# Loading u and v in DMAs of two token tiles each, in a fused attention and maxout kernel

## The chip, the cores and the metric

The kernel runs on one core of a Trainium2 chip. The metric is the device time of one execution in microseconds. A core has five engines that run side by side: TensorE (PE, the matrix unit, with its weight loads shown as PEld), VectorE (DVE), ScalarE (ACT), GpSimd (POOL) and SyncE (SP). POOL and SP also issue the DMAs, which 16 DMA engines carry out.

## The reference

Eight batches of 3072 tokens go through a gated attention without softmax and then through a two-way maxout layer:

```python
scores = (1.0 / S) * np.matmul(z, z.transpose(0, 2, 1))   # z: [8, 3072, 64]
attn = np.maximum(scores, 0.0) ** 2
x = (u * np.matmul(attn, v)).reshape(B * S, D)            # u, v: [8, 3072, 256]
h1, h2 = x @ w1, x @ w2                                   # [256, 1024] each
out = np.maximum(h1, h2) @ w_out                          # [1024, 256]
```

All inputs and the output are float32.

## The kernel before

**Tiling.** A batch is 24 token tiles of 128 tokens. Token `p * 24 + t` lies in partition `p` of tile `t` (`by_tile`, line 68), so neighbouring tiles are neighbours in one partition's row in memory. Four tiles make a group (`G`), two groups a couple: six groups and three couples to a batch. Everything that PE reads is bfloat16. Loads of u, v and z convert on the way in, and POOL issues them.

**u** comes by group: `load_u` (line 181) fills a tile `un` of 128 x 4 x 256 from two buffers in turn, with one DMA. `turn_u` (line 185) then has SP transpose it by DMA into `uT`, which `gate` (line 420) multiplies with the attention's result.

**v** comes in pieces of eight tiles, three pieces a batch, in five buffers: `load_v` (line 151) fills tiles `lo` to `lo + n` of a piece with one DMA. By default that is the whole piece; at the start the first batch's pieces are loaded in parts of 2, 2 and 4 tiles and then of 4. PE reads v as the weights of the attention's product (lines 279 and 892), and DVE's `combine_v` (line 164) forms the differences that the Strassen form needs.

**z** is loaded by `load_z`, except for the first batch, whose z comes in through SP as float32 and is cast by ACT, DVE and, for tiles 12 to 23, POOL (`double_first`, line 118; six casts). PE then transposes it (`zT_pe`, line 122).

**Scores** are made in pairs of token tiles: two matmuls (line 211), a relu on ACT or DVE (lines 222 and 224), a square on DVE (lines 230 and 232). The score matrix is symmetric, so blocks of 512 x 512 above the diagonal are computed and SP mirrors them by DMA transposes (`mirror`, line 261; line 235 inside a diagonal block).

**Stages.** Groups 0 to 3 of the first batch are done plainly, one at a time (loop at line 605). The couple of groups 4 and 5, `i == 2` in the loop at line 740, is the plain couple: four accumulators, two of them on each half of PE's rows at a time, in 96 steps. The 21 couples of the other batches use a Strassen-Winograd form of seven products on 2 x 2 blocks, in 84 steps. After each couple `second` (line 686) runs the maxout layer of the couple before (`ff`, line 435), and its hooks place DVE's work for the next couple.

**Order.** The order of instructions on each engine is written out by hand; semaphores are added from the data that instructions share. In the couples a list `plan` places loads and transposes at step numbers (lines 824 to 866), for example

```python
if i == 2:
    plan = [
        (1, turn_u, 0, 4),
        (4, turn_u, 0, 5),
        (12, load_v, 1, 0),
        (16, load_v, 1, 1),
        (36, load_v, 1, 2),
    ]
```

An accumulator is first added to on one half of PE's rows and later on the other. Between the two, a relay, an instruction that does nothing but wait for the first half's last matmul, has to run on another engine: on POOL in the plain couple, on ACT in all others (line 873). The matmul of the second half waits for the relay (line 904). At a step the relays that are due come before the loads placed there.

POOL's queue therefore holds, in this order of issue: at the start, seven loads of v, the identity matrix, two loads of u, the six casts of z; later the weights, z, u and v, the relays of the plain couple, and all output DMAs (line 476) but the last ten, which SP issues.

Of the kernel before, what the change touches and what calls it, by code (L numbers as in the profile page):

```python
# [11 lines left out]
def kernel(  # L12
# [10 lines left out]
    nc = tc.nc  # L23
# [12 lines left out]
    G = 4  # L36
# [31 lines left out]
    def by_tile(x):  # L68
        return x.rearrange("(p t) d -> p t d", t=NT)
# [81 lines left out]
    def load_v(b, piece, lo=0, n=2 * G, held=False):  # L151
        if (b, piece) not in vp:
            vp[b, piece] = vpool.tile([P, 2 * G, D], bf16, name="v_sb")
        t = vp[b, piece]
        if held:
            nc.vector.memset(t[:, lo, 0:1], 0.0)
        nc.gpsimd.dma_start(
            out=t[:, ds(lo, n), :], in_=by_tile(v[b])[:, ds(piece * 2 * G + lo, n), :]
        )

    def v_at(b, t, dc):
        return vp[b, t // (2 * G)][:, t % (2 * G), ts(dc, P)]
# [16 lines left out]
    un, uT = {}, {}  # L179

    def load_u(b, g):
        un[b, g] = unat.tile([P, G, D], bf16, name="un")
        nc.gpsimd.dma_start(out=un[b, g], in_=by_tile(u[b])[:, ds(g * G, G), :])

    def turn_u(b, g):
        t = upool.tile([P, G, KD, P], bf16, name="uT")
# [360 lines left out]
    def need(b, g, n):  # L547
        most = pair_at[b, g, 2 * g]
        for t in range(n + 1):
            if t // G >= g:  # L550
                most = max(most, pair_at[b, g, t // 2] + 1)
        return most

    with tc.manual_schedule():
# [3 lines left out]
        nc.vector.memset(warm, 0.0)  # L558
        vp[0, 2] = vpool.tile([P, 2 * G, D], bf16, name="v_sb")
        load_v(0, 0, 0, 2)  # L560
        make_identity(nc, ident)
        load_v(0, 0, 2, 2)
        load_v(0, 0, G, G)
        for piece in range(1, NC):
            for lo in (0, G):
                load_v(0, piece, lo, G)
        load_u(0, 0)
        load_u(0, 1)
        z_first += [Block(), Block()]
        w1, w2, w2T = Block(), Block(), Block()  # L570
# [34 lines left out]
        for i in range(PLAIN):  # L605
            b, g = groups[i]
# [3 lines left out]
            for slot, (n, dc) in enumerate(steps_of(i)):  # L610
                tick += 1
                k = need(b, g, n)
# [16 lines left out]
                if i in (1, 2) and n in (5, 8):  # L629
                    k = n // 8  # L630
# [8 lines left out]
                if i + 1 < PLAIN:  # L639
                    if i and n == 1:  # L640
                        load_u(*groups[i + 1])
                    if n == (13 if i == 2 else 16):
                        turn_u(*groups[i + 1])
                if (i, n) in ((0, 20), (1, 10)):
                    w_in = ((w2_sb, moe_w2), (w1_sb, moe_w1)) if i == 0 else ((w_out_sb, moe_w_out),)
                    nc.vector.memset(w_in[0][0][:, 0, 0:1], 0.0)
                    for w_sb, w in w_in:
                        nc.gpsimd.dma_start(
                            out=w_sb, in_=w.rearrange("(c p) f -> p c f", p=P)
# [79 lines left out]
        b, g = groups[PLAIN - 1]  # L729
# [10 lines left out]
        for i in range(PLAIN // 2, len(couples)):  # L740
            b, c = couples[i]
# [3 lines left out]
                b, c, forms, blocks=PLAIN_COUPLES.get(i)  # L745
# [178 lines left out]
        b, c = couples[-1]  # L924
# [31 lines left out]
```

## Time and profile before

| | |
|---|---|
| median of 6 runs | 914.4 us (910.59 to 920.24) |
| the profiled execution | 912.66 us |
| its span, first to last instruction | 910.9 us |
| granted PE clock, mean over the span | 0.998 |
| PE busy | 902.1 us, 99% |
| DVE, ACT, POOL busy | 724.0, 602.0, 105.7 us |
| packets of POOL's DMA queue | 22,592, 52.57 MB, 29.1% of 16 engines' span |
| packets of SP's DMA queue | 359,040, 91.79 MB, 59.8% |
| u loads: number, KB each, us from issue to landing | 48, 256 KB, 6.2 |
| v loads | 21 of 512 KB, 7.2; 5 of 256 KB, 7.3; 2 of 128 KB, 4.6 |

A row of the profile names the engine, the source line, the operation, the tiles (out <- in), the shapes and the count; after the bar come busy time and mean duration, then the engine's idle time before these instructions and what ended it. In the waits, `A L1 <- B L2: 5.0, 3, 2.0` reads: A, before its instruction of line 1, was idle 5.0 us in all in 3 places, 2.0 at most, until B's instruction of line 2 was done. In the stretches each engine's busy time stands with its number of instructions in brackets; then follow the granted clock of PE as a share of full speed, the mean busy share of the 16 DMA engines (packets overlap, so it can pass 1) and the rate. KB are counted as they arrive in the core's memory, so u and v, which halve on the way, take twice that from HBM.

### The profile page before, as it was taken

To read this page: it belongs to the slowest core of one execution; us is meant where nothing else is said; L and a number is where in the kernel's file an instruction comes from. 1 tells how busy PE (TensorE), PEld (TensorE's weight loads), DVE (VectorE), ACT (ScalarE), POOL (GpSimd) and SP (SyncE) were. 2 spreads that over 40 slices of the span, in tenths; PEclk is the share of its full clock that TensorE was granted. 3 is DMA by queue.
4 is the path that set the end of the run, shared out by engine and by line. 5 is a ranking of instruction groups with operands and counts; after the bars stand their busy time and mean duration, and the time that the engine had idled before them with its cause. 6 is when DMAs were issued, how large, how long until landed. Compare 5 with 4: busy or idle time off the path is not lost.

```text
span 910.9 us, 19275 instructions
## 1 busy us (share of the span) xinstructions
PE 902.1 (99%) x7526; PEld 519.8 (57%) x7526; DVE 724.0 (79%) x1093; ACT 602.0 (66%) x1191; POOL 105.7 (12%) x200
## 2 busy tenths in 40 slices
PE   8999999999999999999999999999999999999998
PEld 3456465565565655665656656566465564655655
DVE  6782689779998799887997979979799788995640
ACT  6887966667666676667666666666766567673445
POOL 3101010110110111101111012010110110100000
PEclk9999999999999999999999999999999999999999
DMA  9999989889798895998969999798988979887201
GB/s 190 153 200 205 204 162 171 153 169 191 137 190 146 177 187 112 205 158 165 166 118 204 155 168 180 148 192 148 166 177 143 193 150 181 153 163 142 74 24 71
DMA packets 381724, 145.60 MB, mean 160 GB/s; under 512 B 360256, under 2 KB 364992, under 8 KB 381632
## 3 DMA queue, kind: packets, MB, share of 16 engines
q1 hardware_dynamic: 359040, 91.79, 59.8%
q0 software_dynamic: 22592, 52.57, 29.1%
q8 instruction: 59, 0.97, 0.4%
q14 instruction: 33, 0.27, 0.1%
HBM read 59.77 MB, written 25.17 MB: 93 GB/s over the span
## 4 chain that ended last, share of the span: by engine, by line
PE 97%; DVE 2%; ACT 1%; issue 0%; ACTq 0%; DVEq 0%
PE acc L892 45%; PE d_ps L440 18%; PE o_ps L463 18%; PE s_ps L211 7%; PE o_ps L454 5%; PE acc L279 3%; DVE blk L232 1%; ACT r_sb L224 0%; PE acc L583 0%; DVE blk L230 0%; PE w2o_ps L672 0%; DVE xT L424 0%; DVE w_sb L655 0%; ACT zT L129 0%; PE tpz L125 0%
## 5 line engine op out<-in xcount | busy, mean ns | idle before, releaser
L892 PE MATMUL acc<-blk,v_sb 64*128 64x512 bf16 x2208 | 450.4, 376 | 0.0
L224 ACT ACTIVATE r_sb<-s_ps 128x512 bf16<-128x512 f32 (+3 forms) x672 | 335.9, 559 | 123.3 <-PE s_ps L211 81.9
L892 PE MATMUL acc<-blk,vt 64*128 64x512 bf16 x1512 | 364.1, 376 | 0.0
L892 PEld LDWEIGHTS <-v_sb 64*128 64x128 bf16 x2208 | 176.1, 94 | 133.9 <-issue 6.2
L232 DVE TENSOR_TENSOR blk<-r_sb 128x1024 bf16<-128x1024 bf16 x257 | 172.2, 687 | 92.0 <-ACT r_sb L224 91.0
L447 ACT ACTIVATE g_sb<-d_ps 128x512 bf16<-128x512 f32 x384 | 193.3, 630 | 28.5 <-PE d_ps L440 28.3
L463 PE MATMUL o_ps<-w_out_sb,g_sb 128*128 128x256 bf16 x1536 | 175.5, 273 | 0.0
L892 PEld LDWEIGHTS <-vt 64*128 64x128 bf16 x1512 | 139.2, 94 | 63.0
L440 PE MATMUL d_ps<-xT,w_sb 128*128 128x512 bf16 x768 | 173.9, 379 | 0.0
L463 PEld LDWEIGHTS <-g_sb 128*128 128x128 bf16 x1536 | 150.3, 98 | 17.4
L475 ACT COPY o_sb<-o_ps 128x512 f32<-128x512 f32 (+1 forms) x98 | 56.4, 577 | 132.4 <-PE o_ps L463 132.4
L767 DVE TENSOR_TENSOR h_sb<-h_sb,acc 128x512 f32<-128x512 f32 x168 | 109.3, 681 | 28.7 <-ACT h_sb L771 20.9
L211 PE MATMUL s_ps<-zT 64*128 64x512 bf16 (+3 forms) x676 | 126.4, 360 | 2.4 <-DVE zT L129 1.8
L440 PEld LDWEIGHTS <-w_sb 128*128 128x128 bf16 x768 | 73.3, 98 | 89.3 <-issue 9.7
L476 POOL DMA_DIRECT2D out_dram<-o_sb x88 | 48.1, 546 | 561.6 <-ACT o_sb L475 561.6
L335 DVE TENSOR_TENSOR blk<-blk,blk 128x2048 bf16<-128x2048 bf16 x63 | 77.2, 1225 | 2.1
L331 DVE TENSOR_TENSOR blk<-blk,blk 128x2048 bf16<-128x2048 bf16 x63 | 76.7, 1217 | 0.0
L782 DVE TENSOR_TENSOR blk<-blk,blk 128x2048 bf16<-128x2048 bf16 x63 | 76.5, 1217 | 0.0
L339 DVE TENSOR_TENSOR blk<-blk,blk 128x2048 bf16<-128x2048 bf16 x63 | 73.2, 1217 | 2.5 <-DMA blk<-blk 2.5
L424 DVE SCALAR_TENSOR_TENSOR xT<-h_sb,uT 128x512 bf16<-128x512 f32 x96 | 61.9, 683 | 4.7 <-PE o_ps L454 4.7
L230 DVE TENSOR_TENSOR blk<-r_sb 128x512 bf16<-128x512 bf16 (+3 forms) x162 | 48.3, 334 | 20.2 <-ACT r_sb L224 19.2
L211 PEld LDWEIGHTS <-zT 64*128 64x128 bf16 x676 | 36.0, 94 | 40.7 <-DVE zT L129 2.4
(48 smaller groups left out, 317.1 us busy)
## 6 DMA issues: line engine op xcount, KB each, us to landing
out_dram<-o_sb POOLq DMA_DIRECT2D x88, 256.0 KB, 3.6
un<-in_u_dram POOLq DMA_DIRECT2D x48, 256.0 KB, 6.2
v_sb<-in_v_dram POOLq DMA_DIRECT2D x21, 512.0 KB, 7.2
blk<-blk SPq DMA_TRANSPOSE x240, 4.8
zn<-in_z_dram POOLq DMA_DIRECT2D x21, 128.0 KB, 4.0
out_dram<-o_sb SPq DMA_DIRECT2D x6, 256.0 KB, 2.0
v_sb<-in_v_dram POOLq DMA_DIRECT2D x5, 256.0 KB, 7.3
blk<-in_moe_w_dram POOLq DMA_DIRECT2D x2, 512.0 KB, 6.4
```

The costliest lines, as they stand in the source:

```text
L211: nc.tensor.matmul(s_ps[h][:, lo[h] :], zT[rows, z_at(b, blk * G + tiles[h]), :], zT[rows, q + lo[h] // P : q + G, :].rearrange("p t c -> ...
L224: nc.scalar.activation(o, s, AF.Relu)
L232: nc.vector.tensor_mul(a[:, k : k + 2, :], r, r)
L331: nc.vector.tensor_add(*alike(f["S1"], f["A21"], f["A22"]))
L335: nc.vector.tensor_sub(*alike(f["S2"], f["S1"], f["A11"]))
L339: nc.vector.tensor_sub(*alike(f["S3"], f["A11"], f["A21"]))
L440: nc.tensor.matmul(d_ps, w15_sb[:, kc, ts(nb, P)], xT[:, kc, :], start=(kc == 0), stop=(kc == KD - 1),)
L447: nc.scalar.activation(g_sb[:, nb, :], d_ps, AF.Relu)
L463: nc.tensor.matmul(o_ps[t // 2][:, t % 2, :], g_sb[:, nb, ts(t, P)], w_out_sb[:, nb, :], start=False, stop=(nb == KF - 1 and t % 2 == 1),)
L767: nc.vector.tensor_add(out, a, b_)
L782: nc.vector.tensor_sub(f["A12"].ap, f["A12"].ap, f["S2"].ap)
L892: mm = nc.tensor.matmul(a.out(acc[name]), w()[rows], a.moving(rows, j), start=name not in opened, stop=left[name] == 0,)
```

## The change

Both load functions issue one DMA for every two token tiles, so that one DMA brings 1 KB (2 x 256 bfloat16 values) to each partition. A load of u is two DMAs, a load of a whole piece of v four, a load of half a piece two; the two loads of two tiles at the start stay as they are. Tiles, buffers, places in the order and the waits for a buffer to come free are the same; all DMAs of a load follow one another on POOL.

```diff
@@ -154,9 +154,10 @@
         t = vp[b, piece]
         if held:
             nc.vector.memset(t[:, lo, 0:1], 0.0)
-        nc.gpsimd.dma_start(
-            out=t[:, ds(lo, n), :], in_=by_tile(v[b])[:, ds(piece * 2 * G + lo, n), :]
-        )
+        for k in range(lo, lo + n, 2):
+            nc.gpsimd.dma_start(
+                out=t[:, ds(k, 2), :], in_=by_tile(v[b])[:, ds(piece * 2 * G + k, 2), :]
+            )
@@ -180,7 +181,10 @@
     def load_u(b, g):
         un[b, g] = unat.tile([P, G, D], bf16, name="un")
-        nc.gpsimd.dma_start(out=un[b, g], in_=by_tile(u[b])[:, ds(g * G, G), :])
+        for k in range(0, G, 2):
+            nc.gpsimd.dma_start(
+                out=un[b, g][:, ds(k, 2), :], in_=by_tile(u[b])[:, ds(g * G + k, 2), :]
+            )
```

## The prediction

> **What bounds the kernel now.** I read first the page's busy times and the shares of the chain that ended last, then the waits of TensorE (PE) alone, then GpSimd's (POOL's) groups, because every DMA of the change is issued there, then the start and the one stretch in which PE waits for POOL.
>
> Busy times and chain, from the page:
>
> ```profile
> span 910.9 us, 19275 instructions
> PE 902.1 (99%) x7526; PEld 519.8 (57%) x7526; DVE 724.0 (79%) x1093; ACT 602.0 (66%) x1191; POOL 105.7 (12%) x200
> PE 97%; DVE 2%; ACT 1%; issue 0%; ACTq 0%; DVEq 0%
> ```
>
> PE is the bound from 53 us to the end: 910.9 - 902.1 = 8.8 us are all that any change can give back without shortening matmuls, and the waits of PE alone say that 4.8 us of these lie in the first 53 us:
>
> ```profile
> PE s_ps L211 <- DVE zT L129: 1.8, 1, 1.8
> PE acc L583 <- DVE blk L558: 1.2, 1, 1.2
> PE s_ps L211 <- ACT zT L129: 0.6, 1, 0.6
> PE acc L279 <- DVE blk L232: 0.4, 1, 0.4
> ```
>
> No wait of PE names a DMA. POOL's groups show the price of issuing a load, and what POOL waits for:
>
> ```profile
> L476 POOL DMA_DIRECT2D out_dram<-o_sb x88 | 48.1, 546 | 561.6 <-ACT o_sb L475 561.6
> L183 POOL DMA_DIRECT2D un<-in_u_dram x48 | 26.1, 550 | 97.4 <-DMA uT<-un 96.8 <-issue 0.5
> L157 POOL DMA_DIRECT2D v_sb<-in_v_dram x28 | 15.5, 556 | 41.7 <-PE acc L892 33.6 <-PE s_ps L211 7.3 <-POOLq L940 0.8
> L120 POOL CAST blk<-z 128x256 bf16<-128x256 f32 x6 | 2.3, 481 | 0.0
> ```
>
> POOL is idle for 88% of the span. Two places are not idle time: the start, where six casts that PE needs stand behind nine loads, and the plain couple (84 to 107 us), whose relays (line 873) POOL runs. In time order, POOL and the Vector engine (DVE) at the start:
>
> ```profile
> 2.46 3.21 POOL L157 DMA_DIRECT2D v_sb<-in_v_dram  x6
> 5.63 1.10 POOL L183 DMA_DIRECT2D un<-in_u_dram  x2
> 6.68 2.35 POOL L120 CAST blk<-z 128x256 bf16<-128x256 f32 x6
> 5.95 2.83 DVE L230 TENSOR_TENSOR blk<-r_sb 128x512 bf16<-128x512 bf16 x2
> ```
>
> and the stretches of the granted clock there (columns: stretch, sum of busy time, then PE, PEld, DVE, ACT, POOL, the clock, the DMA share, GB/s):
>
> ```profile
> 6.76:10.17 3.41, 1.57 (x16) 0.71 (x16) 3.21 (x3) 1.40 (x3) 2.27 (x6) 1.00 1.08 189
> 10.17:13.59 3.42, 3.42 (x20) 1.22 (x18) 2.09 (x4) 2.34 (x5) 0.00 (x0) 0.50 1.11 206
> 13.59:17.00 3.41, 2.85 (x30) 1.16 (x26) 1.65 (x3) 2.39 (x4) 0.00 (x0) 1.00 1.19 210
> ```
>
> After a stretch with PE busy 1.57 of 3.41 us the clock is 0.50 for 3.41 us; after one with 2.85 it stays 1.00. Last, POOL's loads in the plain couple and the relays of all couples:
>
> ```profile
> 87.05 0.54 POOL L157 DMA_DIRECT2D v_sb<-in_v_dram  x1 [2.53 <-PE s_ps L211]
> 88.13 0.54 POOL L157 DMA_DIRECT2D v_sb<-in_v_dram  x1 [0.54 <-PE acc L892]
> 93.39 0.53 POOL L157 DMA_DIRECT2D v_sb<-in_v_dram  x1 [4.72 <-PE s_ps L211]
> ...
> L873 ACTq EVENT_SEMAPHORE  x126: 17/17/17, 128.2 to 870.5; - x126
> L873 POOLq EVENT_SEMAPHORE  x44: 17/17/17, 84.2 to 106.8; - x44
> ```
>
> **The change part by part.** *Count.* 48 loads of u become 96; of the 28 loads of v, 21 whole pieces become four each (+63), five half pieces two each (+5), two loads of two tiles stay. That is 116 more DMAs, 116 x 0.55 = 64 us of POOL. They lie in the 561.6 us that POOL waits for o_sb: each burst of loads starts right after an output DMA, and the next output comes 5 us or more later (22 to 25 us in most cases). Cost 0 there. If that cover were gone, an output would be late by at most the 3 + 1 + 1 extra issues of a burst, 2.7 us.
>
> *The relays.* In the plain couple PE repeats every 1.08 us: the last matmuls of two accumulators on one half of the array, then POOL's two relays, then the matmuls on the other half that wait for them. One by one, the trace has relays at 84.23 and 84.32 and the waiting matmuls at 84.90, so the second relay may be 0.58 us late. Loads of v stand in POOL's order after the relays of steps 12, 16 and 36. Behind the relay of 86.48 the load's record begins at 87.05, 0.57 later; loads in a row begin 0.53 apart (the start above: 3.21 us for six), and POOL's sequencer is held until the last has begun. Today that is free by 87.05, ahead of the next relays at 87.47 and 87.56. With four loads it is free at 0.57 + 3 x 0.53 = 2.16 us after the relay, the second relay comes at 2.25, and PE wants it at 1.08 + 0.58 = 1.66: PE stalls 0.6 us. The load of step 16 stands behind those late relays: its own next pair comes 2.25 after them, while PE, which resumed on them, wants it 1.08 later: 1.2 us. The load of step 36 stands alone again: 0.6. Sum 2.4 us. Bounds: 0 if queued DMAs do not hold the sequencer (the single loads here do not delay a relay); above, each POOL DMA carries one of eight semaphores in turn and waits for the eighth before it. The last DMA of the step 16 load would wait for the output issued at 83.97, which landed 6.0 us later, at 89.96; its turn is about 90.3. Were that landing 1 us later, 0.7 more. So 0 to 3.1, and I take 2.4, by the row that is nearest.
>
> *The start.* POOL now issues 9 loads by 6.15 and then the casts. It will issue 16 ahead of them, and the last waits for the landing of the eighth. Loads of 256 KB landed 1.25 us apart here (8.87 to 15.13 us), the second of the 128 KB ones at 7.36, so the eighth lands at 7.36 + 6 x 0.63 = 11.1, or 12.0 if each takes 0.78. The casts then begin at 12.2 to 13.1 and the fourth ends 1.5 later, at 13.7 to 14.6; PE's transposes that need it ran at 14.21. So 0 to 0.4 later. But the casts leave 6.7 to 9.0, where one DVE instruction of line 230 took 2,272 ns beside them (346 is the line's median) and PE then idled 1.84 us. Without that PE is earlier at first, then waits for the casts, and the slow 3.41 us of clock may come after instead of before them. Between a gain of 0.8 (ScalarE's copy of zT was 0.6 to 0.8 us late for other work, and could start earlier) and a loss of 1.5 (the slow stretch falls where PE had 2.85 us of work), I take 0, in the middle.
>
> *The transfers.* The list of packets has 4,096-byte packets of 266 ns on average (v among the stores), 2,048-byte ones of 213 (u) and 1,024-byte ones of 126 (z). Rows of 1 KB make u cost 6,144 x (2 x 126 - 213) = 0.24 ms and v 2,688 x (4 x 126 - 266) = 0.64 ms more, some 0.9 ms over 16 engines: 55 us of each, 6% of the span, on shares that already exceed 1.0 in places (1.08 to 1.19 above). What must land in time: v's last piece has 3.3 to 5.1 us between landing and DVE's line 171 (555.2 against 558.5 is the tightest), and becomes later by 1.6 of issue and 8 x (504 - 266) ns = 1.9 of packets, 3.5 at most. u has 8 us and more to its transpose from 139 us on; before that 0.07 to 2.7, for three or four transposes on SyncE (SP), and the mirror transposes queued behind them, by 0.5 to 1 us each. Only one wait of the whole trace names a mirror (2.5 us, DVE line 339). Cost 0; without that cover up to 1 us for each of seven batches, and less than 0 is excluded, since PE waits for no transfer.
>
> [...]
>
> *Waits.* Each quarter brings its own semaphore to the matmuls, transposes and DVE instructions that read it. PE has one extra semaphore instruction at line 892, of 51 ns; 68 of these would be 3.5 us, 0 if a free wait slot or the weight loads' lead hides them. With one in all the couples I take 0.3, near that end.
>
> Sum: 2.4 + 0 + 0 + 0.3 = 2.7 us. The profiled execution took 912.66 us (910.9 of span, 1.8 around), so 915.4; it stands 1.7 below the median of six, 914.4, so the forecast is 917.1. Its own range, with the start from -0.8 to 1.5 and the relays from 2.4 to 3.1, is 916.0 to 919.3. All lower ends together give 913.6; all upper ends together, the seven batches' 7 and the 3.5 of waits among them, 929.5.
>
> **The rivals.**
> *The clock closes behind the stalls (slower).* The stretch with 1.84 us idle cost the next one half its clock. A stall of 1.2 in 3.41 leaves 2.2 busy, between the 1.57 that closed it and the 2.85 that did not; 0.6 and 1.2 in one stretch leave 1.6. Each closing costs 3.41 / 2 = 1.7: 918.8 with one, 920.5 with two. It decides from the second. [...]
> *The transfers become the bound (slower).* Landings grow beyond v's 3.3 to 5.1 us. For it: DMA shares above 1; against: no wait on DMA today. 5.4 us later is 0.7 x 7 batches = 5 us more: 922. It decides from about 5 us of delay.
> *The relays are not held.* For it: single loads delay none. Against: the issue rhythm of 0.53. Then 914.4 + 0.3 = 914.7.
> *The start gains.* The 1.84 idle us go, and the casts come in time: 917.1 - 1.7 = 915.4.
>
> **How the numbers follow.** Forecast 0.38, clock 0.24, transfers 0.12, relays not held 0.14, start gains 0.12. Slower by over 0.5% (4.6 us; about what this kernel's runs can tell) is two thirds of the clock's case (with a late start or two closings), all of the transfers' and a tenth of the forecast's: 0.16 + 0.12 + 0.04 = 0.32. Faster by 4.6 us would need more than half of PE's idle time back: 0.02. The rest, 0.66, is within. The range runs from 913.0 (relays not held and the start's gain) to 922.5 (two closings and a late start, 922.0, or the transfers' point).
>
> **What would show it.** POOL with 316 instructions and 170 us busy; stalls of PE at line 892 of 0.6, 1.2 and 0.6 us between 88 and 96 us, with the relays after three rows of four loads; POOL's casts at 12 to 14 us and line 230 back under 0.5 us; no new PE wait after 108 us; some 37,400 packets on POOL's queue. I am wrong if PE waits for DMA in the Strassen couples, if the clock's row shows 0.50 after 17 us, or if the relays keep their 1.08 us.

## The result, and the profile after

The changed kernel takes 918.77 us in the median of 35 runs (913.23 to 930.66), the kernel before, in 72 runs beside it, 916.6 (909.4 to 941.77). The ratio is 1.0041 with a 95% interval from 1.0021 to 1.006: the change costs 3.8 us (1.9 to 5.5), where 2.7 were forecast. The direction and the size of the whole were right; two of the terms were not, and the profiles show which.

Single runs of either kernel differ by 17 to 32 us, and the ratios here and below leave out runs over 1.5% above the fastest of their kernel, so they are not the ratio of the two medians (1.0024). The lowest times, 913.23 against 909.40, are again 3.8 apart. The profiled execution of the changed kernel, 924.36 us, is 5.6 above its own median, while the one of before (912.66) is 3.9 below that of the 72 runs. What the two profiles differ by, 11.7 us, is therefore a long execution beside a short one; it shows the mechanism well, and its size badly.

The page of the changed kernel, with span, busy times and the chain:

```profile
span 922.6 us, 19475 instructions
PE 903.1 (98%) x7526; PEld 519.5 (56%) x7526; DVE 722.3 (78%) x1093; ACT 602.0 (65%) x1191; POOL 167.7 (18%) x316
PE 90%; issue 5%; DMA 2%; POOL 1%; ACT 0%; DVE 0%; ACTq 0%; POOLq 0%
```

PE's own waits:

```profile
PE acc L896 <- POOLq L877: 9.9, 2, 9.3
PE tpz L125 <- POOL blk L120: 2.7, 2, 2.4
PE acc L587 <- DVE blk L562: 1.2, 1, 1.2
```

PE's busy time has hardly changed (902.1 and 903.1). Two waits have come that were not there: for POOL's relays in the plain couple (line 877 was 873) and for POOL's casts at the start. The two waits for zT (1.8 and 0.6) have shrunk to one of 0.4. The chain has 1% on POOL, where it had none. The groups show POOL's price and the room that it still has:

```profile
L480 POOL DMA_DIRECT2D out_dram<-o_sb x88 | 48.1, 547 | 528.5 <-ACT o_sb L479 528.5
L185 POOL DMA_DIRECT2D un<-in_u_dram x96 | 51.6, 558 | 81.9 <-DMA uT<-un 78.7
```

POOL is busy 62 us more with issuing, but it still waits 528.5 us for o_sb. The plain couple on POOL, in time order:

```profile
85.95 1.62 POOL L158 DMA_DIRECT2D v_sb<-in_v_dram  x3 [2.53 <-PE s_ps L215]
87.87 0.53 POOL L158 DMA_DIRECT2D v_sb<-in_v_dram  x1 [0.30 <-DMA un<-in_u_dram]
90.56 1.05 POOL L158 DMA_DIRECT2D v_sb<-in_v_dram  x2 [2.15 <-DMA un<-in_u_dram]
97.79 1.16 POOL L158 DMA_DIRECT2D v_sb<-in_v_dram  x2 [6.18 <-DMA out_dram<-o_sb]
```

and PE beside it:

```profile
88.03 0.82 PE L896 MATMUL acc<-blk,v_sb 64*128 64x512 bf16 x6 [0.61 <-POOLq L877]
98.57 1.03 PE L896 MATMUL acc<-blk,v_sb 64*128 64x512 bf16 x4 [9.29 <-POOLq L877]
```

Of the four DMAs of step 12, three begin 0.53 us apart; the fourth waits 0.30 us for a load of u to land, and PE stalls 0.61 us behind them. Those of step 16 do not follow each other: the first waits 2.15 us for an earlier load of u to land, the third 6.18 us for an output. Meanwhile the relays behind them stand still, and PE with them for 9.29 us. The load of step 36, four DMAs from 105.08 on, follows without a stall of the matmuls. The output that POOL waits for is the one issued at 81.08, eight DMAs earlier: it landed 16.4 us later, and the chain that ended last runs through it. The two outputs issued at 81.08 and 82.87 took nearly three times as long to land as in the kernel before. For the outputs issued from 80 to 86 us, the kernel before had

```profile
DMA to landing us min/median/max: 5.6/5.8/6.0
```

and the changed kernel

```profile
DMA to landing us min/median/max: 15.3/15.8/16.4
```

The stretches of the changed kernel, cut where the clock's own stretches begin (the columns are those of the prediction), first two at the start and then those of the stall:

```profile
8.26:11.67 3.41, 2.21 (x18) 0.74 (x14) 2.81 (x5) 3.05 (x6) 2.68 (x6) 1.00 1.23 200
11.67:15.08 3.41, 1.77 (x17) 0.77 (x18) 0.57 (x1) 1.01 (x1) 2.54 (x7) 1.00 1.25 204
90.17:93.58 3.41, 0.00 (x0) 0.00 (x0) 0.69 (x1) 0.01 (x1) 1.05 (x2) 1.00 1.36 129
93.58:97.00 3.42, 0.00 (x0) 0.00 (x0) 0.00 (x0) 0.00 (x0) 0.00 (x0) 0.50 1.37 132
97.00:100.41 3.41, 1.84 (x10) 0.73 (x12) 0.00 (x0) 0.00 (x0) 1.06 (x2) 0.50 1.24 166
100.41:103.82 3.41, 3.41 (x20) 1.21 (x16) 0.77 (x2) 2.17 (x4) 0.00 (x0) 0.50 1.41 83
```

Behind the empty stretch the clock is 0.50 for three stretches, 10.2 us. PE had 1.84 + 3.41 = 5.25 us of work in them, of which half, 2.6, is lost: the matmuls with v are busy 453.0 us on the page (line 896), 450.4 before (line 892), and a pair of scores takes 0.63 us there and 0.38 behind it.

Three landmarks of PE split the difference of the two profiles. The first matmul of the maxout layer begins at 67.2 us before and 66.1 after; the second block of this layer, after the plain couple, at 108.5 and 120.2; the last at 891.2 and 902.9. So the start gave 1.1 us in this pair, the plain couple took 54.1 - 41.3 = 12.8 (9.9 of stalls and 2.6 of clock), and the 21 Strassen couples took 782.7 us in both: nothing. 12.8 - 1.1 = 11.7.

### The profile page after: what moved, and what is told of

Read it like the earlier page. It is cut to its first block, busy times and chain, and to the rows that moved or that the text cites. A ratio compares the mean times of both kernels' runs of the same rounds, so it can differ in the third digit from the quotient of the medians.

```text
span 922.6 us, 19475 instructions
## 1 busy us (share of the span) xinstructions
PE 903.1 (98%) x7526; PEld 519.5 (56%) x7526; DVE 722.3 (78%) x1093; ACT 602.0 (65%) x1191; POOL 167.7 (18%) x316
## 2 busy tenths in 40 slices
DMA packets 398429, 145.62 MB, mean 158 GB/s; under 512 B 362112, under 2 KB 391168, under 8 KB 398336
## 3 DMA queue, kind: packets, MB, share of 16 engines
q0 software_dynamic: 39296, 52.58, 32.6%
## 4 chain that ended last, share of the span: by engine, by line
PE 90%; issue 5%; DMA 2%; POOL 1%; ACT 0%; DVE 0%; ACTq 0%; POOLq 0%
PE acc L896 44%; PE d_ps L444 17%; PE o_ps L467 17%; PE s_ps L215 6%; PE o_ps L458 4%; DMA out_dram<-o_sb 2%; PE acc L283 1%; POOL un L185 1%; DMA v_sb<-in_v_dram 0%; POOL v_sb L158 0%; DVE blk L236 0%; POOL blk L120 0%; POOL zn L135 0%; ACT r_sb L228 0%; POOL out_dram L480 0%
## 5 line engine op out<-in xcount | busy, mean ns | idle before, releaser
L896 PE MATMUL acc<-blk,v_sb 64*128 64x512 bf16 x2208 | 453.0, 378 | 9.9 <-POOLq L877 9.9
L480 POOL DMA_DIRECT2D out_dram<-o_sb x88 | 48.1, 547 | 528.5 <-ACT o_sb L479 528.5
L185 POOL DMA_DIRECT2D un<-in_u_dram x96 | 51.6, 558 | 81.9 <-DMA uT<-un 78.7
L234 DVE TENSOR_TENSOR blk<-r_sb 128x512 bf16<-128x512 bf16 (+3 forms) x162 | 46.2, 321 | 20.2 <-ACT r_sb L228 19.2
```

The lines of the kernel that those rows point to most:

```text
L896: mm = nc.tensor.matmul(a.out(acc[name]), w()[rows], a.moving(rows, j), start=name not in opened, stop=left[name] == 0,)
```

## The experiments

The theory was that POOL's queue alone is what costs: the relays behind the loads in the plain couple, and the casts behind the loads at the start. The rivals were the transfers themselves (more and smaller packets, all through the kernel), and the transposes of z, which the page counts on the same 16 DMA engines (before, SP's queue takes 59.8% of their time and POOL's 29.1%). The kernels only_plain, all_but_plain, only_start and couples_only split the change in parts, the other runs took single causes away. In all, `step` is the number of token tiles in one DMA; diffs are against the changed kernel unless they say otherwise, and leave out the lines that only put `step` in the place of 2. The profile of only_plain has a mean granted clock of 0.949; a pair of scores takes 0.39 to 0.40 us in its plain couple, 0.38 in the kernel before.

| kernel | loads in several DMAs | median | before, same chip | ratio, 95% | lowest | before's lowest |
|---|---|---|---|---|---|---|
| changed | all | 918.77 | 916.60 | 1.0041, 1.0021 to 1.006 | 913.23 | 909.40 |
| only_plain | v of the plain couple | 916.39 | 917.22 | 0.9991, 0.9948 to 1.0034 | 911.95 | 909.59 |
| all_but_plain | all others | 920.35 | 917.22 | 1.0019, 0.9976 to 1.0061 | 912.81 | 909.59 |
| only_start | nine loads at the start | 919.74 | 917.22 | 1.0016, 0.9972 to 1.0059 | 912.51 | 909.59 |
| relays_act | all, relays on ACT | 922.32 | 917.22 | 1.0043, 0.9994 to 1.0092 | 911.42 | 909.59 |
| before_early_z | none, z's transpose earlier | 919.24 | 920.80 | 1.001, 0.996 to 1.006 | 910.49 | 909.82 |
| after_early_z | all, z's transpose earlier | 920.06 | 920.80 | 1.0037, 1.0004 to 1.007 | 915.15 | 909.82 |
| plain_two | all, the plain couple's v in halves | 916.36 | 917.47 | 1.0007, 0.9964 to 1.005 | 911.92 | 909.60 |
| before_late_v | none, the plain couple's v later | 918.04 | 917.47 | 1.0013, 0.997 to 1.0056 | 909.51 | 909.60 |
| couples_only | only those of the Strassen couples | 919.48 | 917.90 | 1.0003, 0.9951 to 1.0055 | 911.12 | 910.55 |

Each of the experiments has 12 runs. Their intervals are some 0.4% to each side, as wide as what is looked for; only those of the changed kernel and of after_early_z leave out 1. What tells the versions apart is the waits in their profiles, and, less surely, the lowest times: 12 of the 35 runs of the kernel before that ran beside the first four, taken at random, would have a lowest time of 910.0 on average, 0.4 above that of all 35.

### Only the plain couple's loads of v (only_plain)

```diff
-        for k in range(lo, lo + n, 2):
+        step = 2 if b == 1 else n
+        for k in range(lo, lo + n, step):
...
-        for k in range(0, G, 2):
+        step = G
+        for k in range(0, G, step):
```

> Only the three loads of v in the plain couple are split, into four DMAs each; all other loads are whole. Theory 'relays': the whole loss sits here, PE waits in line 896's place for POOL's relays, 0.6 us for the first load and 1.2 to 9.3 us for the second (the more, the later the output DMA eight places before lands), and the start is as before (DVE's 2.3 us instruction, 1.84 us of PE idle, clock 0.50 from 10.2 to 13.6 us). The change cost 0.41% with a start that was some 1.1 us faster, so this should cost 0.41% + 0.12%: ratio 1.005, between 1.003 and 1.010. Rival 'packets' (finer DMAs make transfers dearer everywhere): 9 of 116 added DMAs, so 0.03%: ratio 1.000.

POOL in the plain couple of only_plain:

```profile
86.00 4.26 POOL L159 DMA_DIRECT2D v_sb<-in_v_dram  x8 [2.66 <-PE s_ps L217]
93.78 1.70 POOL L159 DMA_DIRECT2D v_sb<-in_v_dram  x3 [3.52 <-PE s_ps L217]
95.94 0.53 POOL L159 DMA_DIRECT2D v_sb<-in_v_dram  x1 [0.46 <-DMA v_sb<-in_v_dram]
```

and PE's wait in it:

```profile
PE acc L898 <- POOLq L879: 1.5, 2, 1.0
```

Here POOL waits for no output: the two landed within 7.2 us. Eight DMAs go out in 4.26 us, and the relays behind the last of them come late by the issue time alone: PE stands 0.97 us there, and not at all behind the first four. The other 0.57 us, behind the load of step 36, follow a wait of 0.46 us for an earlier load of v to land (the third row). This is the relay term without late outputs, 1.5 us of it in the waits and 2.4 in the lowest times (1.9 with the allowance above). The ratio missed what was expected: it was to be 1.003 to 1.010, and 0.9991 is the rival's value. By itself it would have shown nothing.

### All but those (all_but_plain)

```diff
-        for k in range(lo, lo + n, 2):
+        step = n if b == 1 else 2
+        for k in range(lo, lo + n, step):
```

> All loads of u and v are split except the three of v in the plain couple. Theory 'relays': no PE wait for POOL after the start; what stays is the start's gain of about 1.1 us: ratio 0.9988, between 0.997 and 1.000. Rival 'packets': 107 of 116 added DMAs, so 0.38%: ratio 1.004, with the loss spread over waits of the Strassen couples.

The waits of PE in it:

```profile
PE s_ps L216 <- DMA zT<-zd: 5.1, 1, 5.1
PE tpz L125 <- POOL blk L120: 2.4, 1, 2.4
```

and three stretches from its start on:

```profile
9.03:12.44 3.41, 1.59 (x14) 0.44 (x8) 3.24 (x5) 2.43 (x5) 2.92 (x6) 1.00 1.24 202
12.44:15.86 3.42, 2.74 (x16) 1.28 (x18) 0.00 (x0) 1.01 (x1) 1.92 (x6) 0.50 1.22 199
15.86:19.27 3.41, 3.41 (x18) 1.22 (x16) 1.38 (x2) 1.11 (x3) 0.00 (x0) 0.50 1.19 174
```

The relays no longer stall PE, and a wait of 5.1 us has come in their place: PE stands before the scores for which z of the next batch must be transposed. That transpose is issued by SP. In the first profile of before it landed at 90.05 us, and the weight load that reads it began at 90.09, after 0.35 us of waiting for it: it had nothing to spare. The waits of PE's matmuls do not say so; those of its weight loads do:

```profile
PEld L211 <- DMA zT<-zd: 0.4, 1, 0.4
```

The expected gain of the start did not come (ratio 1.0019, 0.997 to 1.000 expected), and the lowest time is 3.2 us above that of before. The wait for the casts stays, and with 1.59 us of work in its stretch the clock closes for two.

### Only the start (only_start)

```diff
-        for k in range(lo, lo + n, 2):
+        step = 2 if b == 0 else n
+        for k in range(lo, lo + n, step):
...
-        for k in range(0, G, 2):
+        step = 2 if (b, g) in ((0, 0), (0, 1)) else G
+        for k in range(0, G, step):
```

> Only the first batch's loads of v and the first two loads of u are split (the 16 DMAs ahead of POOL's casts). Theory 'start': the casts move from 6.7 to about 11.7 us, DVE's instruction of line 230 falls from 2.27 to under 0.5 us, PE's idle 1.84 us at 9.4 goes and the clock is 1.00 from 10.2 to 13.6 us, but PE then waits some 2.7 us for the casts; net gain 1.1 us, ratio 0.9988. Rival 'no gain': the clock closes after the wait for the casts and takes 1.7 us back, ratio 1.000 to 1.001.

The start was expected to gain, and by the lowest time it loses; the ratio, 1.0016, cannot tell. PE waits for the casts as long as in the changed kernel:

```profile
PE tpz L125 <- POOL blk L120: 2.8, 2, 2.5
```

The lowest time is 2.9 us above that of before (2.5 with the same allowance). Why the forecast missed this shows in the repeated look at the kernel before, below.

### The relays on ACT (relays_act, relays_act_again)

```diff
-                    relays[name] = (nc.gpsimd if plain else nc.scalar).nop()
+                    relays[name] = nc.scalar.nop()
```

> All loads are split as in the changed kernel, but the plain couple's relays run on ACT instead of POOL. Theory 'relays': loads on POOL can wait as long as they like, PE does not; ACT is busy 22.8 of 24 us in that couple with activations of 0.6 us, and the relay has 0.58 us to spare, so at most a few tenths of us of waits take the place of the stalls: ratio 0.9985 to 1.001. Rival 'packets': nothing that it blames is touched, ratio 1.004 as for the changed kernel.

> All loads split, the plain couple's relays on ACT, for a second profile: its first was at the fast end of its runs, and showed no stall in the plain couple. Theory: no wait of PE for POOL or ACT relays here either; if the run is over 915 us, PE waits for DMA zT<-zd instead, as in the unsplit kernel's slow runs. Rival: ACT's relays stall PE, and the row names ACT.

POOL in the plain couple of relays_act:

```profile
83.61 2.69 POOL L158 DMA_DIRECT2D v_sb<-in_v_dram  x5
86.66 0.53 POOL L158 DMA_DIRECT2D v_sb<-in_v_dram  x1 [0.35 <-DMA un<-in_u_dram]
89.65 1.13 POOL L158 DMA_DIRECT2D v_sb<-in_v_dram  x2 [2.47 <-DMA out_dram<-o_sb]
91.49 1.14 POOL L158 DMA_DIRECT2D v_sb<-in_v_dram  x2 [0.70 <-DMA v_sb<-in_v_dram]
```

and its engines in that time:

```profile
85.00:95.00 10.00, 10.00 (x96) 4.48 (x92) 6.23 (x9) 9.57 (x19) 5.01 (x10) 1.00 1.21 200
```

The DMAs still wait for the landing of earlier ones, 2.47 us for an output, but nothing that PE needs stands behind them: it works 10.00 of 10.00 us at full clock. That shows that the stall is made by the order on POOL's queue and not by late data of v. What is left is the start (a wait of 2.8 for the casts), and the lowest time, 911.42, is 1.8 above that of before and 1.8 below that of the changed kernel. The ratio and the median go against this: 1.0043, the rival's value, where at most 1.001 was expected, and 922.32, above the median of the changed kernel. Both profiles of this version, spans 909.6 and 910.5, are clean, so what makes most of its runs 10 us longer was not seen, and stays open.

### Both kernels once more (before_again, after_again)

> The kernel before, for a second profile. Single times of one kernel spread over 20 us and more, in the kernel before too. Theory 'late z': the spread comes from one spot, PE's score matmuls of the second batch, whose first zT transpose landed at 90.05 us in the first profile and was read at 90.09: where it lands later, PE waits in the plain couple and the clock closes behind it. In a run over 912 us there is then a wait of PE for DMA zT<-zd between 85 and 105 us; in a run under 911 none over 0.5 us. Rival: the spread is the chip's clock alone, with no such wait in a slow run. For the start: where the 1.84 us of PE idle fall into two of the clock's 3.41 us stretches, no 0.50 follows and line 279 reaches the point of 24.3 us in the first profile some 2 to 3 us earlier.

> The changed kernel, for a second profile. Theory 'relays': PE again waits for POOL's relays at the v loads of the plain couple, at least 0.6 and 1.2 us, and as much as 9 us where the output DMA eight places before lands late; POOL's row before the third or fourth DMA of the second load names out_dram. Rival: the 9.3 us of the first profile were an accident of another kind, and no wait for POOL stands there.

The second profile of the kernel before has another start than the first:

```profile
5.80 0.75 DVE L230 TENSOR_TENSOR blk<-r_sb 128x512 bf16<-128x512 bf16 x2
```

and, in its stretches,

```profile
6.76:10.17 3.41, 2.95 (x27) 1.31 (x26) 2.66 (x4) 3.00 (x6) 3.09 (x7) 1.00 1.09 192
10.17:13.59 3.42, 3.03 (x30) 1.26 (x28) 2.61 (x5) 2.65 (x5) 0.00 (x0) 1.00 1.12 199
```

The two DVE instructions take 0.75 us together, where they took 2.83 in the first profile; PE is busy 2.95 us in the first stretch instead of 1.57, and the clock does not close. The pair was done at 6.55 us here, before POOL's casts began:

```profile
6.80 3.05 POOL L120 CAST blk<-z 128x256 bf16<-128x256 f32 x6
```

In the first profile the pair began 0.15 us later and ran into the casts, which began at 6.68. The first maxout matmul begins at 63.9 us instead of 67.2. It begins at 63.9, 64.9 and 64.4 in the other kernels with an undivided start (before_early_z, before_late_v, couples_only), and at 66.1 to 68.8, 67.3 on average, in the eight profiles with a divided one. So among five profiles with an undivided start and the full clock, the first one's was the only bad one. Its 2.3 to 3.3 us were not there to be given back in the others, and against those the divided start loses 3.0 us on average. The wait for the casts shows in PE's transposes, here and in the first profile of the changed kernel:

```profile
10.56 0.62 PE L125 MATMUL tpz<-ident,blk 128*128 128x128 bf16 x8
12.89 0.40 PE L125 MATMUL tpz<-ident,blk 128*128 128x128 bf16 x4 [2.42 <-POOL blk L120]
```

The theory that a late z makes the long runs was not borne out: this run took 912.63 us, over the 912 above which a wait for zT was expected, and PE's matmuls show no such wait. No run of the kernel before over 913 us was profiled, so what makes its long runs stays open; in versions of it a late z does show in long runs (before_early_z, 918.41 us, below).

The second profile of the changed kernel has the stalls in other sizes:

```profile
PE acc L896 <- POOLq L877: 4.5, 1, 4.5
PE tpz L125 <- POOL blk L120: 2.7, 2, 2.4
```

and POOL in its plain couple:

```profile
87.50 2.68 POOL L158 DMA_DIRECT2D v_sb<-in_v_dram  x5 [2.53 <-PE s_ps L215]
93.15 0.53 POOL L158 DMA_DIRECT2D v_sb<-in_v_dram  x1 [1.40 <-DMA out_dram<-o_sb]
100.99 2.12 POOL L158 DMA_DIRECT2D v_sb<-in_v_dram  x4 [5.91 <-PE s_ps L215]
```

The outputs landed within 9.8 and 10.2 us there, and the stall is 4.5 instead of 9.3. The load of step 12 (the first four DMAs of the first row) waits for no landing, and PE's scores behind it come 1.25 us apart instead of 1.08: it costs 0.17 us. The load of step 36 (the last row) costs the matmuls nothing. From the first maxout block to the second it took 48.5 us, against 41.3 and 41.4 in the kernel before, and from the second to the last 785.2, against 782.7 and 785.1.

### The transpose of z earlier (before_early_z, after_early_z)

Against the kernel before, and the same edit in the changed one:

```diff
-                if (i, n) in ((2, 8), (3, 10)):
+                if (i, n) in ((2, 8), (3, 4)):
```

> The kernel before, with the second z transpose of the second batch placed six tile steps earlier, ahead of SP's mirrors. Theory 'late z': PE no longer waits for zT in the plain couple, and the runs between 912 and 940 us become fewer: median 910 to 913 against 917, ratio 0.992 to 0.997. Rival 'clock alone': nothing changes, ratio 0.998 to 1.002, same spread.

> The changed kernel with the same early z transpose. Theory: zT's wait goes here too, and what is left over the kernel before with early z is the relays' 2.4 us and the start's 1.8 us (the undisturbed runs: 911.5 of span against 907.8): some 4 us more than that kernel, median 914 to 917. Rival 'packets': the split loads make z late by themselves, so that with z early no difference is left: median within 1.5 us of the kernel before with early z.

It was to take away the wait for zT, and moved it to the next transpose. Of before_early_z:

```profile
PE s_ps L211 <- DMA zT<-zd: 7.4, 1, 7.4
```

PE reads this later zT at 103.42 us. So the transposes of z can be late in this whole time, without any load divided, and not by the place of one of them. In after_early_z the order on POOL stalls PE again, 3.7 us with outputs that land within 9.1 and 10.2. Neither is faster than what it was made from (before_early_z was to have a ratio of 0.992 to 0.997, and has 1.001). Whether the early z leaves a difference between the two is not clear: by the medians (919.24 and 920.06) it does not, as the rival said; by the lowest times (910.49 and 915.15) it does, as the theory said.

### The plain couple's v in halves (plain_two)

```diff
-        for k in range(lo, lo + n, 2):
+        step = G if b == 1 else 2
+        for k in range(lo, lo + n, step):
```

> All loads split as in the changed kernel, but the three loads of v in the plain couple are two DMAs of four tiles each instead of four of two. Theory 'relays, by hold and eighth DMA': two DMAs hold POOL's sequencer 0.57 + 0.53 = 1.1 us after the relay, inside the 1.66 us that PE allows, and the DMA eight places before is then a load of u, not an output, and has landed: PE waits 0 to 0.3 us for POOL (3.7 to 9.3 us in three profiles with four DMAs). The split start stays: the first maxout matmul is at 66 to 69 us as with all split starts, against 63.9 to 67.2 whole. Ratio 1.001 to 1.004. Rival 'any split in the plain couple stalls': at least half of the stall stays, 2 us or more of PE waiting for POOL.

POOL in its plain couple:

```profile
87.58 2.15 POOL L159 DMA_DIRECT2D v_sb<-in_v_dram  x4 [2.53 <-PE s_ps L216]
93.88 1.06 POOL L159 DMA_DIRECT2D v_sb<-in_v_dram  x2 [4.15 <-PE s_ps L216]
```

PE waits for no relay. A load of two DMAs holds the queue for 0.57 + 0.53 = 1.1 us by the prediction's reckoning, less than the 1.66 after which PE wants the second relay; and none of the six DMAs had to wait for the landing of another. Which of the two does it is not shown by this run: four DMAs in a row were nearly free as well where none waited for a landing (0.17 us and nothing in the second profile of the changed kernel). What stalled PE by 0.5 us and more was eight DMAs in close order (0.97 in only_plain) or a DMA that waits for a landing, and the halves have neither.

### The plain couple's v later (before_late_v)

Against the kernel before:

```diff
-                    (12, load_v, 1, 0),
-                    (16, load_v, 1, 1),
-                    (36, load_v, 1, 2),
+                    (50, load_v, 1, 1),
+                    (60, load_v, 1, 0),
+                    (70, load_v, 1, 2),
```

> The kernel before with the three loads of v in the plain couple at steps 50, 60 and 70 instead of 12, 16 and 36. Theory 'mixed traffic': where POOL's loads and SP's transposes run together both fall to a fraction of their rate (transposes 147 to 218 GB/s alone, 1 to 100 beside loads), which makes the z transposes late in many runs of every version. With the loads out of the way until the z transposes have landed, PE waits for no zT: fewer runs above 912 us, median 911 to 914, ratio 0.993 to 0.998, and no wait for the v loads at DVE's line 171 (115 us). Rival: the spread has another source, ratio 0.999 to 1.002.

Moved out of the time in which z is transposed, the loads leave a wait of 0.5 us for zT, but the median and the lowest time are those of before (the ratio was to be 0.993 to 0.998, and is 1.0013). This is no better kernel either; none was found that beats the kernel before.

### Only the Strassen couples (couples_only)

```diff
-        for k in range(lo, lo + n, 2):
+        step = n if b < 2 else 2
+        for k in range(lo, lo + n, step):
...
-        for k in range(0, G, 2):
+        step = G if (b, g) in ((0, 0), (0, 1)) else 2
+        for k in range(0, G, step):
```

> Both parts that the earlier runs blame are undone at once: the start's loads (first batch's v, first two u) and the plain couple's three loads of v are whole, everything else (the later 18 pieces of v, 46 loads of u; 100 of the 116 added DMAs) is split. Theory 'start and relays alone': PE waits neither for POOL's casts nor for POOL's relays, the first maxout matmul is back at 64 to 67 us, the stretch from the second maxout stage to the end takes 782 to 785 us as everywhere, runs under 912 us are seen again, and the ratio is 0.998 to 1.002. Rival 'packets': 86% of the added DMAs are still there, so 86% of the loss: ratio 1.0035, and no run under 912 us.

100 of the 116 added DMAs are kept, and the ratio is 1.0003. Of PE's waits, those for casts and relays are gone; the first is that for z's transpose, seen above without divided loads too:

```profile
PE s_ps L217 <- DMA zT<-zd: 2.1, 1, 2.1
```

The lowest time is 0.6 above that of before on the same chip. The interval, 0.9951 to 1.0055, would hold the rival's 1.0035 as well; the profiles decide. From the second maxout block to the end of the span it takes 802.0 to 802.4 us in eleven profiles at the full clock, seven of them with divided loads in the couples and four without; the two repeats took 805.6 (before) and 804.9 (changed). So the loss lies ahead of that block. How it divides is less sure: by the lowest times the relays cost 2.4 us (only_plain) and everything else 1.8 (relays_act) or 3.2 (all_but_plain), which makes 4.2 to 5.6 from the parts, against 3.8 for the change as a whole.

## Why the prediction was right, and where not

**The count and POOL's room.** Right. POOL has 316 instructions and 167.7 us (170 forecast), and the couples, where most of the added DMAs lie, cost nothing. The packets of POOL's queue are 39,296 and not 37,400; the difference is about 16 small ones for each added DMA, 1,856, which the forecast left out (packets under 512 B went from 360,256 to 362,112).

**The relays.** Right in place and in the kind of wait; the sizes were not. The forecast holds the relays back until the last DMA of a load has begun. They can pass earlier: behind four DMAs in a row the next relay passed 0.2 us after the third had begun and 0.3 before the fourth (at 106.34 us in the first profile of the changed kernel, between 106.12 and 106.64; in the second the weight load that waits for it ran at 88.96, where the fourth began at about 87.50 + 3 x 0.53 = 89.1). So a load that stands alone costs 0.17 us or nothing, where 0.6 was forecast twice. That the first stall measured 0.61 is luck: in that profile the fourth DMA, and the relays with it, waited for a load of u to land. The load of step 16, forecast as 1.2, costs 0.97 by issue time alone (only_plain). With that the lower bound, that queued DMAs do not hold the sequencer, fell. The upper bound was mis-sized the other way, "were that landing 1 us later, 0.7 more". It named an output (the long wait was for the one before it, in front of the third DMA of the load), and then took its landing of 6.0 us in one profile as if it could move by 1. The outputs landed after 9.8 to 16.4 us in the profiles of the changed kernel, and the stalls were 4.5 and 9.9 us in place of 2.4 to 3.1. Why they land so late is not settled: with the same DMAs and the relays on ACT, they landed after 6.9 to 8.1.

**The start.** The term was 0, between -0.8 and 1.5; it is a loss of about 1.8 to 2.9 by the lowest times, 3.0 by the first maxout matmul. Some steps held: the casts ran at 11.7 us (12 to 14 forecast, a little early), and DVE's line was back to 0.75 us for two. What failed was the base. The 2,272 ns and the slow stretch of clock in the profile of before were taken as the state of that kernel, to be given back by the change, and they show in one of five profiles. So the casts were compared with transposes at 14.21 us and found 0 to 0.4 late; in an undisturbed start these transposes run at 10.56, and in the changed kernel PE waits for the casts until 12.89, 2.42 us.

**The transfers.** 0 is right for the Strassen couples, 782.7 us in both first profiles. The packets were dearer, by less than was forecast: POOL's queue went from 29.1% to 32.6% of 16 engines' span, where 6% more was reckoned. The reason given, that PE waits for no transfer, was not quite true even of the first profile, where a weight load waited 0.35 us for z's transpose; in other versions, with loads divided or not, PE waits up to 7.4 us for it. The two profiles of the changed kernel show at most 0.3 of this wait in the matmuls, where POOL's stall lies just ahead of it. That the one stands in for the other, and that the ratio is therefore only 0.4% although these profiles lost 7 to 13 us in this couple, fits all of them, but was not tested by itself.

**The extra semaphores**, 0.3 in the sum: no trace of them in the couples; 0 is as good.

**The rivals.** That the clock closes behind the stalls has come true in both profiles of the changed kernel, with 0.50 for 10.2 us in the first and 6.8 in the second, but as a consequence of one long stall and not of two short ones: 0.61 us did nothing. That transfers become the bound is refuted by the 802.0 to 802.4 us from the second maxout block on, with and without divided loads. That the relays are not held is refuted by only_plain. That the start gains held in the pair of first profiles (1.1 us) and in the lowest time of no version. Of the three signs named for being wrong, the clock's (0.50 after 17 us) appeared, so the forecast's account of the stall was too mild. Its total came out right partly by luck: the start's term was too small, and the relays' 2.4 us are neither the 1.1 or so of the issue time alone (0.17 + 0.97) nor the 4.5 and 9.9 with late outputs.

## What to carry to other kernels

With instructions that only pass a signal on the queue that also issues the DMAs, PE waited 9.9 and 4.5 us for them in the two profiles here; with the same instructions on ACT it waited for none in either profile. So before a load on such a queue is split, compare the time it holds the queue (here 0.53 us a DMA, and the landing of the DMA issued eight before) with the time after which the signal is wanted (here 1.66 us). A baseline profile of one execution tells which waits occur and not which are usual, so a loss that the change is to give back should be seen twice, and the slack of each transfer before its reader should be read from the trace, the waits of the weight loads among it, even where the list of PE's matmuls is silent.

## What was not expected of the hardware

**The clock.** In the traces of the kernel before and of the changed one, the granted clock changes only after 3.41 us or a whole multiple of it (it is 0.50 for 3.41 us in the first and for 10.24 in the second). In the stretches looked at, up to the last couple, 0.50 came behind those in which PE worked 0.00 us (the changed kernel), 0.96 (its second profile), 1.26 (relays_act_again), 1.57 (before) and 1.59 (all_but_plain), and 1.00 behind 1.77, 1.91 and 2.21 (the changed kernel). Where it was 0.50, it was so again after 1.84 (the changed kernel) and 2.74 (all_but_plain), and 1.00 after 3.02 (relays_act_again), 3.14 (the second profile of the changed kernel) and 3.41. What happens between 1.59 and 1.77 is not shown by these. The start of the changed kernel idles 2.42 us in one piece without a loss, where a border of two stretches cuts it in 1.20 and 1.22; in all_but_plain a wait of 2.4 us leaves 1.82 us idle in one stretch and costs two at half clock.

**DMAs that wait for DMAs.** In the traces of the kernel before and of the changed one, POOL's DMAs (188 and 304) carry the semaphores 99 to 106 in turn, and none of them begins before the one issued eight before it has landed. In the changed kernel seven waited for that, 0.23 to 6.18 us, for two loads of v, two of u, one of z and two outputs; the longest is the load of v behind the output of 81.08. The wait shows among POOL's own waits; PE's waits name only the relay behind it.

**DVE beside POOL's casts.** In the first profile of before, one of a pair of DVE instructions took 2,272 ns while the casts ran (346 is its line's median); in the second the pair was done before the casts and took 0.75 us together. In before_late_v the casts met two instructions of line 232 instead, and these took 2.85 us together, where one takes 0.69 on average. In these three profiles the pair began at 5.95, 5.80 and 5.95 us and the casts at 6.68, 6.80 and 7.54, so tenths of a us at the start went with which instructions of DVE took longer beside the casts, and by how much. The 1.9 us that the first one lost are longer than one cast, 481 ns; how the casts slow DVE was not shown. Issuing DMAs on POOL did not slow DVE: its instructions of line 236 take 0.69 us in the changed kernel at its first uses, beside DMA issues, and 687 ns on average.
